# Scores of two units in a row from unit 7 on, in the first batch of an attention and gated-MLP kernel

## Chip and metric

One core of one Trainium2 chip. The metric is device time in microseconds (us) of one execution; "before" is the kernel below, "after" the same kernel with the change. The engines are TensorE (PE; its weight loads PEld), VectorE (DVE), ScalarE (ACT), GpSimd (POOL) and SyncE (SP, which here only issues DMAs).

## What is computed

```python
# q (8,16,384,64), k and v (8,4,384,64): 4 query heads share one k/v head
scores = (1/sqrt(64)) * q @ k.T
attn   = softmax(scores)            # over the 384 keys
x      = (attn @ v)                 # -> (8, 384, 1024)
h      = relu(x @ w_in)             # (8, 384, 1024); u, v = halves of 512
v_n    = (v - mean(v)) / sqrt(var(v) + 1e-6)
v_s    = w_spatial @ v_n + b_spatial   # along the 384 positions
out    = (u * v_s) @ w_out
```

All inputs and the output are float32; the kernel computes its products in float16 with float32 sums.

## The kernel before

**Units.** Work is divided by batch b (8), by *set* s of a batch (6: three blocks of 128 query positions qt, and two halves j of the heads, s = 2 qt + j), and by block kt of 128 keys (3). A *unit* u is one (b, s, kt): u = 18 b + 3 s + kt. `units` (L267) makes its scores: two matmuls of 64 x 128 by 64 x 512 (`sc`, L281), one for each half hh of the array's rows, each into a PSUM bank of its own. The two run at the same time on the two halves of the array. `exp` (L291) then has ACT take the exponential of each into a tile `aT` (L293), which frees the bank. There are three buffers of aT, one for a set.

**What hangs on the units.** When the three units of a set are done, `weigh` (L295) multiplies with v, once for each hh: 12 matmuls (`av`, L301) into one bank; VectorE takes a reciprocal (L315) and a product (`x`, L317), which frees the bank. Here av(s,hh) stands for the one of set s. `x_turn` (L328) transposes x on PE (`xps`, L334, four transposes, two of them of each hh) for the dense part; VectorE copies it out (L218). `q_turn` (L234) does the same for the queries of a set (`qps`, L240), which the scores of that set read as `qT`; `k_turn` (L220) for the keys (`kps`). From batch 2 on, q and k are turned by DMA instead, sent from SP's queue (`q_send`, `k_send`), and from batch 1 on x (`x_send`, L338). The sends of batch 2 are emitted from step 24 on.

**The dense part** is a generator, `gated` (L514), that yields after each matmul: v_part (`pv`, L357, 8 matmuls, then VectorE makes `vr`, L371, and `measure`, L378, its statistics `bn_stats`, L383, right after the next weigh), u_part (`pu`), s_part (`psp`), o_part (`po`). `pour` (L727) takes matmuls from it until a given time in ns is used up; an item ("from", n) stops it until step n. In batch 0 the half v_parts are held so until steps 7, 10, 13, 16, 19.

**Order.** The order on every engine is the order in which this program emits (L53, a manual schedule). In the first 21 units it is one loop with a step per unit:

```python
for u in range(ALONE):                              # ALONE = 21
    if u < TWO or (u - TWO) % 2 == 0:
        pairs = units(u, 1)
        if u >= TWO and u + 1 < ALONE:
            pairs += units(u + 1, 1)
        for pair in pairs:
            exp(*pair)
    spare = 736 if u < TWO else (600 if (u - TWO) % 2 == 0 else 870)
```

After this, in each step: the step's listed work (`todo`; q_turn of set (qt, j) = (1,1) at step 6, (2,0) at 10, (2,1) at 12; x_turn at 5, 9, 12, 15, 18; casts of q on VectorE at step 8; each turn takes 224 off `spare`), the weighs that have become due (for set s of batch 0 at steps 3 s + 4 and 3 s + 5; set 0 both at 4; each takes 372 off), and a pour of what is left of `spare`. From unit 21 on, a second loop takes three units in a row.

**PSUM banks.** All eight banks are shared. `bank` (L79) takes the one that a running estimate expects to be free first:

```python
i = min(range(8), key=done.__getitem__)
t = ps.tile(shape, dtype, name=name, tag=f"bank{i}")
```

The estimate only chooses. On the chip a matmul that writes a bank waits until the engine that reads its earlier content is done.

Of the kernel before, what the change touches and what calls it, by code (L numbers as in the profile page):

```python
# [18 lines left out]
def kernel(  # L19
# [247 lines left out]
    def units(u, count):  # L267
        b, r = divmod(u, UNITS)
        s, kt0 = divmod(r, NT)
        qt, j = divmod(s, 2)  # L270
        kts = range(kt0, kt0 + count)
        if kt0 == 0:
            aTs[b, s] = att.tile([P, NT, 2, G * P], FP16, name=f"aT_{b}_{s}", tag="aT", bufs=3)
        scs = [
            (kt, hh, bank([P, G * P], FP32, f"sc_{b}_{s}_{hh}_{kt}"))
            for hh in range(2)
            for kt in kts
        ]
        for kt, hh, sc in sorted(scs, key=lambda x: x[:2]):
            rows = slice(hh * D, (hh + 1) * D)  # L280
            nc.tensor.matmul(  # L281
                sc,
                kTs[b][rows, j, kt * P : (kt + 1) * P],
                qTs[b, j][rows, qt].rearrange("p (r i c) -> p i r c", r=G, i=G),
                start=True,
                stop=True,
            )
        spend(count * C512 + 186)
        return [(aTs[b, s][:, kt, hh], sc, f"sc_{b}_{s}_{hh}_{kt}") for kt, hh, sc in scs]

    def exp(a, sc, name):  # L291
        reads(act, 480.0, name)
        act.activation(a, sc, AF.Exp, scale=scale)  # L293
# [451 lines left out]
    F = (0.2, 0.3, 0.1, 0.4)  # L745
    owed = 0.0
    halves = {}
    TWO = 13
    for u in range(ALONE):
        if u < TWO or (u - TWO) % 2 == 0:  # L750
            pairs = units(u, 1)
# [5 lines that stand above are left out]
        for f, args in todo.pop(u, []):  # L757
# [282 lines left out]
```

## Time and profile before

| | |
|---|---|
| median of 3 runs | 238.40 us (238.39 to 239.18) |
| the profiled execution | 238.65 us, of which its span 237.1 us |
| busy PE, ACT, VectorE, POOL | 97%, 72%, 61%, 43% |
| granted TensorE clock | 1.00 |
| `sc`, one matmul (288 of them) | 380 ns |
| exponential of 128 x 512 (288) | 617 ns |
| `av`, one matmul (1152) | 193 ns |
| `x`, one product (96) | 424 ns |

The span runs from the first to the last instruction of the program. A row of a timeline gives the start in the span, the length, the engine, the line, and what was written from what; rows with the same line that follow each other are merged, with their number (x4). Rows of PE overlap, since matmuls are pipelined: what a row costs is the distance to the start of the next. Mean lengths in the table overlap too.

The first 21 units lie between 6.2 and 27.8 us. Units 7 to 12 take from 12.5 to 19.2 us.

### The profile page before, as it was taken

The page shows a single profiled execution, that of the slowest core. Times are in us where ns is not written, and L with a number is a line of the kernel's source. Part 1 is how long each engine was busy: PE and PEld are TensorE (multiplying, and loading weights), DVE is VectorE, ACT ScalarE, POOL GpSimd, SP SyncE. Part 2 cuts the span into 40 slices and gives each one's busy share as a digit, 9 for nine tenths or more (in the row PEclk, how much of TensorE's full clock was granted, in tenths as well). Part 3 has the DMA queues.
Part 4 walks back from the last instruction along what each step waited for, and adds up shares of the span by engine and source line. Part 5 has one row for each costly group of instructions (what it writes and reads, how often), then busy time and mean ns, then how long its engine had stood idle before and what let it go on. Part 6 is the DMA issues. An engine that isn't in the chain of part 4 may idle for free.

```text
span 237.1 us, 5954 instructions
## 1 busy us (share of the span) xinstructions
PE 230.4 (97%) x2317; PEld 124.3 (52%) x2317; DVE 143.8 (61%) x382; ACT 170.0 (72%) x350; POOL 102.2 (43%) x149
## 2 busy tenths in 40 slices
PE   7899999999999999999999999999999999999993
PEld 6555655545554545555464555554465455545542
DVE  2668774676447674566646576376744667367561
ACT  2899989959897869977797776986697776401212
POOL 3489493642556442275045800575032500460740
PEclk9999999999999999999999999999999999999999
DMA  6999959999999999699988899479912543240266
GB/s 186 289 300 308 275 152 160 169 317 260 296 211 237 258 351 171 214 199 309 188 257 214 241 214 294 68 271 158 255 27 44 114 164 79 48 177 0 86 229 222
DMA packets 67757, 47.48 MB, mean 200 GB/s; under 512 B 48368, under 2 KB 60576, under 8 KB 67728
## 3 DMA queue, kind: packets, MB, share of 16 engines
q1 hardware_dynamic: 62800, 39.86, 68.9%
q0 software_dynamic: 3952, 6.42, 12.3%
q10 hardware_dynamic: 976, 0.82, 1.1%
q8 instruction: 18, 0.29, 0.5%
q14 instruction: 11, 0.09, 0.1%
HBM read 25.95 MB, written 12.58 MB: 163 GB/s over the span
## 4 chain that ended last, share of the span: by engine, by line
PE 91%; DMA 4%; DVE 2%; issue 0%; ACTq 0%; ACT 0%
PE pu L438 18%; PE pv L357 17%; PE po L496 17%; PE sc L281 15%; PE av L301 14%; PE psp L457 7%; DMA q<-in_q_dram 2%; DMA qT<-q 2%; PE qps L240 1%; PE xps L334 1%; DVE x L317 1%; DVE qT L218 0%; DVE osb L218 0%; DVE q L208 0%; ACTq L124 0%
## 5 line engine op out<-in xcount | busy, mean ns | idle before, releaser
L293 ACT ACTIVATE aT<-sc 128x512 f16<-128x512 f32 x288 | 147.5, 617 | 31.4 <-PE sc L281 30.8
L301 PEld LDWEIGHTS <-aT 128*128 128x128 f16 x1152 | 47.0, 97 | 17.3 <-issue 2.3
L357 PE MATMUL pv<-w_in,xt 128*128 128x512 f16 x192 | 51.0, 380 | 0.1
L301 PE MATMUL av<-v,aT 128*128 128x65 f16 x1152 | 50.5, 193 | 0.1
L496 PE MATMUL po<-w_out,gT 128*128 128x512 f16 (+2 forms) x200 | 50.5, 371 | 0.0
L438 PE MATMUL pu<-xt,w_in 128*128 128x384 f16 x256 | 49.9, 327 | 0.0
L401 POOL TENSOR_SCALAR vn<-vr,rstd,nmr 128x512 f16<-128x512 f32 x23 | 17.6, 779 | 67.0 <-DVE nmr L396 45.6
L474 POOL TENSOR_TENSOR gT<-vs,uT 128x384 f16<-128x384 f32 x31 | 32.4, 1058 | 31.8 <-DVE r_all L315 16.9
L317 DVE TENSOR_TENSOR x<-av,r_all 128x256 f16<-128x256 f32 x96 | 40.7, 424 | 3.3
L281 PE MATMUL sc<-qT,kT 64*128 64x512 f16 x288 | 41.5, 380 | 0.3
L315 DVE RECIPROCAL r_all<-av 128x4 f32<-128x4 f32 x96 | 17.1, 178 | 40.6 <-PE av L301 40.3
L218 DVE COPY osb<-po 128x512 f32<-128x512 f32 (+2 forms) x39 | 26.1, 669 | 16.3 <-PE po L496 16.3
L438 PEld LDWEIGHTS <-w_in 128*128 128x128 f16 x256 | 22.1, 98 | 17.1 <-issue 5.5
L449 ACT ACTIVATE uT<-pu 128x384 f16<-128x384 f32 x32 | 15.8, 495 | 16.0 <-PE pu L438 15.8
L496 PEld LDWEIGHTS <-gT 128*128 128x128 f16 x200 | 17.6, 98 | 17.1 <-issue 3.3
L357 PEld LDWEIGHTS <-xt 128*128 128x128 f16 x192 | 15.8, 97 | 17.8 <-issue 5.5
L281 PEld LDWEIGHTS <-kT 64*128 64x128 f16 x288 | 10.9, 94 | 23.5 <-issue 11.9
L457 PE MATMUL psp<-wsT,vn 128*128 128x384 f16 x96 | 22.2, 327 | 0.0
L469 DVE TENSOR_TENSOR vs<-psp,bias_bc 128x384 f32<-128x384 f32 x32 | 17.6, 552 | 7.1 <-PE psp L457 6.9
L371 DVE TENSOR_SCALAR vr<-pv 128x512 f32<-128x512 f32 x24 | 16.4, 682 | 8.4 <-PE pv L357 8.3
L203 POOL CAST q<-q 128x768 f16<-128x768 f32 x22 | 17.6, 830 | 7.9 <-issue 4.3
L383 DVE BATCH_NORM_STATS2 stats<-vr 128x6 f32<-128x512 f32 x24 | 16.4, 685 | 0.1
(55 smaller groups left out, 103.2 us busy)
## 6 DMA issues: line engine op xcount, KB each, us to landing
out_dram<-osb SPq DMA_DIRECT2D x20, 512.0 KB, 3.9
q<-in_q_dram SPq DMA_DIRECT2D x10, 768.0 KB, 5.7
v_None<-in_v_dram SPq DMA_DIRECT2D x6, 384.0 KB, 7.0
w_in<-in_moe_w_in_dram POOLq DMA_DIRECT2D x4, 512.0 KB, 9.8
k_None<-in_k_dram SPq DMA_DIRECT2D x5, 384.0 KB, 3.8
out_dram<-osb SPq DMA_DIRECT2D x7, 256.0 KB, 2.5
q<-in_q_dram POOLq DMA_DIRECT2D x2, 768.0 KB, 7.6
w_out<-in_moe_w_out_dram POOLq DMA_DIRECT2D x2, 512.0 KB, 9.5
```

The source lines that it names most:

```text
L203: eng.tensor_copy(t16[:, :, :, hh, :], src[:, hh])
L218: (act.copy if eng is act else dve.tensor_copy)(o, i)
L281: nc.tensor.matmul(sc, kTs[b][rows, j, kt * P : (kt + 1) * P], qTs[b, j][rows, qt].rearrange("p (r i c) -> p i r c", r=G, i=G), start=True ...
L293: act.activation(a, sc, AF.Exp, scale=scale)
L301: nc.tensor.matmul(av[:, i * (D + 1) : (i + 1) * (D + 1)], aT[:, kt, hh, i * P : (i + 1) * P], v1[b % 2][:, 2 * j + hh, kt, 0 : D + 1], st ...
L317: dve.tensor_tensor(x16s[b][:, qt, c : c + 256].rearrange("p (i d) -> p i d", i=G), o[:, :, 0:D], r.to_broadcast([P, G, D]), ALU.mult,)
L357: nc.tensor.matmul(pv, xts[b][:, kt, st * P : (st + 1) * P], w_in16[:, kt, DH:DFF], start=(kt == 0), stop=(kt == NK - 1),)
L401: (dve if b == 0 and st == 1 else pool).tensor_scalar(vn, v_r.pop((b, st)), rstd[:, st : st + 1], nmr[:, st : st + 1], op0=ALU.mult, op1=A ...
L438: nc.tensor.matmul(pu[:, 0:S], w_in16[:, kt, m * P : (m + 1) * P], xts[b][:, kt, :], start=(kt == 0), stop=(kt == NK - 1),)
L457: nc.tensor.matmul(psp[:, 0:S], v_n[b, st][:, m * P : (m + 1) * P], wsT16[:, st, :], start=(st == 0), stop=(st == NT - 1),)
L474: pool.tensor_tensor(gT, vs, uT, ALU.mult)
L496: nc.tensor.matmul(po[:, 0:width], gTs[b][:, m, tt * P : (tt + 1) * P], w_out16[:, m, c0 : c0 + width], start=(m == 0), stop=(m == NM - 1),)
```

## The change

```diff
     F = (0.2, 0.3, 0.1, 0.4)
     owed = 0.0
     halves = {}
-    TWO = 13
+    TWO = 7
     for u in range(ALONE):
         if u < TWO or (u - TWO) % 2 == 0:
             pairs = units(u, 1)
```

`TWO` is the first unit that is taken together with its successor. Before, units 0 to 12 are taken one in a step, and 13 and 14, 15 and 16, 17 and 18, 19 and 20 two in the odd steps. After, this begins with 7 and 8: the scores of 8, 10 and 12 are emitted one step earlier, right behind those of 7, 9 and 11, with their four exponentials behind them, and steps 8, 10 and 12 have no scores. The time that is poured in steps 7 to 12 becomes 600 and 870 in turn, where it was 736 each.

## The prediction

> **What bounds the kernel now.** I read the page first, for the engine that carries the chain.
>
> ```profile
> PE 230.4 (97%) x2317; PEld 124.3 (52%) x2317; DVE 143.8 (61%) x382; ACT 170.0 (72%) x350; POOL 102.2 (43%) x149
> ...
> PE 91%; DMA 4%; DVE 2%; issue 0%; ACTq 0%; ACT 0%
> ```
>
> PE is the bound. PE time taken off early reaches the end unless a later wait for something else gives it back; a wait added on PE is added to the end likewise. So I read PE's timeline through steps 7 to 12 (the start of a row minus the start of the next is what it costs on the chain; the second column overlaps):
>
> ```profile
> 12.18 0.40 PE L240 MATMUL qps<-ident,q 128*128 128x128 f16 x4
> 12.51 0.39 PE L281 MATMUL sc<-qT,kT 64*128 64x512 f16 x2
> 12.83 0.54 PE L301 MATMUL av<-v,aT 128*128 128x65 f16 x12
> 13.20 0.59 PE L357 MATMUL pv<-w_in,xt 128*128 128x512 f16 x2
> 13.73 0.39 PE L281 MATMUL sc<-qT,kT 64*128 64x512 f16 x2
> ...
> 18.64 0.39 PE L334 MATMUL xps<-ident,x 128*128 128x128 f16 x4
> 18.87 0.38 PE L357 MATMUL pv<-w_in,xt 128*128 128x512 f16 x1
> 19.18 0.61 PE L281 MATMUL sc<-qT,kT 64*128 64x512 f16 x4
> 19.72 0.54 PE L301 MATMUL av<-v,aT 128*128 128x65 f16 x12
> ```
>
> Units 7 (12.51) and 8 (13.73) stand apart; units 13 and 14 (19.18) stand together. No row has PE idle. Then the engines that free the banks: VectorE's timeline.
>
> ```profile
> 12.61 0.42 DVE L218 COPY qT<-qps 128x512 f16<-128x512 f16 x1 [0.23 <-PE qps L240]
> ...
> 14.85 0.42 DVE L317 TENSOR_TENSOR x<-av,r_all 128x256 f16<-128x256 f32 x1
> ...
> 17.98 0.42 DVE L317 TENSOR_TENSOR x<-av,r_all 128x256 f16<-128x256 f32 x1
> ```
>
> The qps copy holds its bank until 13.03, the two x products hold theirs until 15.27 and 18.40. Today nobody waits for these three; the change moves PE work in front of all of them. ACT in this stretch starts an exponential every 477 ns while it has a backlog (units 3 to 8, up to 14.75), and catches up afterwards (gaps of 0.21 us before unit 9, 0.19 before unit 12): it sets bank times, but not the pace.
>
> **What the change saves.** No instruction is added or removed; the order on PE and what is poured between change. A lone unit costs 0.32 us from its start to the next row (12.51 to 12.83), a pair of units 0.54 (19.18 to 19.72): a second unit in a row is 0.22, so leaving a score group costs 0.32 - 0.22 = 0.10. Two pv products before a score group take 0.53 (13.20 to 13.73), before anything else 0.43 (24.38 to 24.81): entering costs 0.10 too. Three groups go (8, 10 and 12 join 7, 9 and 11): 3 x 0.20 = -0.60 us.
>
> The Trainium skill prices such a break otherwise: its page "TensorE: Matmul & The Clock Gate", section "Single matmul latency", gives a lone warm matmul (398 + N)/2.4 ns, so 398/2.4 = 166 ns beside the streaming. By it three breaks would be an estimated 0.50 us and the sum below 0.10 higher; the row's 0.20 decides.
>
> **What it adds: waits for banks.** I wrote out the loop's order by hand, with the kernel's rule for banks (the one whose planned release is earliest) and its pouring. The same writing-out for the kernel before gives the timeline's order row for row. From step 21 on both orders are the same and each bank follows the same use, so all differences lie in steps 7 to 21:
> 7: sc7 sc8 av(1,0) 2 pv; 8: av(1,1) 2 pv; 9: sc9 sc10 xps; 10: qps av(2,0) 2 pv; 11: sc11 sc12 av(2,1) 1 pv; 12: qps xps 1 pv; 13: sc13 sc14 av(3,0) 2 pv; 14: av(3,1) 2 pv; 16 to 20: pv 2, 1, 1, 1, 1 (before 1, 2, 0, 2, 1).
>
> *Step 7.* Unit 8's second matmul gets the bank of step 6's qps, the only one due. It is due at 12.51 + 0.22 = 12.73; the copy ends at 13.03, and a matmul starts 0.05 after its bank comes free (27.92, where the vr before it ended at 27.19 + 0.68 = 27.87). **+0.35**, start 13.08. Behind it on PE are queued av(1,0) at 13.40, av(1,1) at 13.40 + 0.37 + 0.43 = 14.20, unit 9 at 14.20 + 0.37 + 0.53 = 15.10 (14.96 before).
>
> *Step 9.* Unit 10's second matmul gets av(1,1)'s bank, due 15.32. av(1,0) being later, VectorE has reciprocal 13.97, x 14.19, the two casts of step 8 from 14.53 (0.42), reciprocal of (1,1) 14.95, x 15.17 to 15.59; +0.05. **+0.32**. Then xps 15.96, qps 16.19, av(2,0) 16.42, unit 11 at 17.32 (16.86 before), unit 12 at 17.54. Unit 12 also reads the qT that step 10's qps feeds: PE ends that at 16.59, VectorE copies it behind the xt copy, 16.72 to 17.14, so 0.35 us of cover is left; without it a delay of that copy counts in full.
>
> *Step 12.* av(2,1) starts at 17.86; x ended 1.22 after its av before (17.18 to 18.40), so 19.08. The two pv and the score group that stood between are now one pv: xps starts at 18.69, its third transpose is due at 18.80 and needs that x: 19.13. **+0.33**. Unit 13 at 19.55 (19.18 before).
>
> *Step 18.* Likewise: before, x of (4,1) ended at 25.22 and the third transpose came at 25.31, 0.04 after it could. One pv less stands between: **+0.18**.
>
> *Step 21.* Between unit 19 and unit 21 stand two pv, not three: 2.24 us (25.52 to 27.76) become 2.02. The exponentials of unit 20 end 2.00 and 2.48 after unit 19's start in the records (27.52 and 28.00). Unit 21's second matmul takes the first one's bank (+0.03), unit 22's second the other's: 2.53 against 2.27 (+0.26). Unit 23's second follows step 20's qps, whose copy now stands behind bn_stats (0.69 us, and 0.18 for its aggregate): +0.22. A wait of 0.16 before (27.76 to 27.92, for vr) goes, as that pv ends earlier. **+0.35**.
>
> Sum: -0.60 + 0.35 + 0.32 + 0.33 + 0.18 + 0.35 = **+0.93 us** from unit 24 on, +0.9 in round numbers. Bounds of each wait: nothing, if the planner's bank came free sooner, and the sum of all is 1.53; so -0.60 to +0.93, and I stand at the upper end because the three ends on VectorE are rows, and each lies behind the point where PE will stand.
>
> **What is late next.** From step 21 to 54 us PE's few gaps (30.4, 31.6) wait for work that PE itself started, so they move with it. Then come the queue of SP and PE's own rows:
>
> ```profile
> 31.94 1.41 SPq L586 DMA_TRANSPOSE wsT<-ws  x1
> 33.99 1.24 SPq L341 DMA_TRANSPOSE xt<-x  x1
> ...
> 42.44 0.58 SPq L124 DMA_DIRECT2D q<-in_q_dram  x1
> ...
> 50.10 1.23 SPq L258 DMA_TRANSPOSE qT<-q  x1
> ```
>
> ```profile
> 54.33 0.63 PE L301 MATMUL av<-v,aT 128*128 128x65 f16 x12
> 55.08 1.11 PE L281 MATMUL sc<-qT,kT 64*128 64x512 f16 x6
> ```
>
> The chain has "DMA qT<-q" from 50.10 to 55.04: unit 42 waits there 0.28 us (an av before a score group takes 0.37 + 0.10, so 54.80 was due). Does that wait give back? Its DMA hangs on the q load issued at 42.44, behind the transposes on SP, and these follow the xt send at 33.99, which waits for an x product, so for PE: SP had been free since 33.35. The landing moves with PE; I take nothing back. Bounds: 0 to 0.28 given back. No step of POOL's or SP's program is moved past another: their work is emitted at steps 2, 3 and from 20 on. Afterwards the chain is PE up to the last copy.
>
> **Forecast.** The profiled execution: 238.65 + 0.9 = 239.55 (span 238.0). It stands 0.25 over the median of 238.4; the median goes to 239.3. A measurement of this kernel tells about 0.5%, 1.2 us, from no change (one of three runs was 239.18), so this is slower by less than can be told. Own range: 0.93 - 0.28 = +0.65 to +1.1 (terms rounded up): 239.0 to 239.5.
>
> **Rivals.** *The banks come free in time.* Then only -0.60 is left, 237.8; with the wait at 55.08 shortened too, 237.5. For it: the first transposes and copies on VectorE might be done a little earlier than the records' ends, and ACT's backlog holds no bank that is asked for in steps 7 to 12. Against: three rows with fixed ends, and PE must pass them in order. The Trainium skill's same page, section "The mechanism", says that matmuls start and end strictly in order and only weight loads are pulled ahead: by that rule the av behind the waiting score cannot fill the hole; the trace agrees where unit 21 waits (27.92: the next rows move with it). It decides if the fourth matmul of 12.51's group starts before 12.85.
>
> *The delay runs into the weights' transfer.* POOL issues 1 MB of w_out at 34.14 and 34.88 by its own time, landing at 42.0 and 46.1. Before, the xt transposes are mostly through when it begins at about 36.2 (q1 moved some 550 packets per us from 33 to 37, and under 50 per us from 37 to 41). Started 0.9 later they leave some 500 packets behind it, which at the 210 per us of 41 to 46 is up to 2.4 us for kT, qT and the q load behind them. kT and qT of batch 2 land at 46.5 and 47.0 for use at 48.1, so they are covered; the qT of 55.04 would land up to 2.4 later while PE is there 0.9 later: +0.3 to +1.8 beyond what the forecast has, 239.6 to 241.1, middle 240.4. It decides when xt lands more than 0.9 later than its 40.5. For it: the page's DMA row is full from 37 on. Against: SP itself was held by those same packets until 40.7 before, so the q load need not move more.
>
> **Chances.** Forecast 0.60, banks in time 0.14, transfer 0.26. Of the forecast 0.07 passes +1.2 by the spread of runs; of the banks' rival 0.04 passes -1.2. Faster 0.04, slower 0.26 + 0.07 = 0.33, same 0.63. The range 238.0 to 240.6 leaves out most of the banks' rival (0.11) and the transfer's top (0.09).
>
> **What would show it.** In the changed profile: four scores from 12.5 whose last starts near 13.08; av(1,0) at 13.4; a second such hole near 15.6; an xps near 18.7 with its third transpose 0.33 late; unit 13 near 19.55, unit 21 near 28.3 with two holes, unit 24 near 32.0; the qT landing near 55.9. Wrong: unit 13 before 19.2 (the waits do not bite), or unit 42 later than 56.3 (the transfer).

## The result, and the profile after

| | before | after |
|---|---|---|
| median | 238.44 us (22 runs, 237.77 to 239.42) | 239.21 us (22 runs) |
| ratio after / before | | 1.0029, 95% interval 1.0016 to 1.0043 |
| profiled execution, span | 238.65, 237.1 us | 239.49, 237.9 us |
| first `sc` of unit 7 / unit 24 | 12.51 / 31.07 us | 12.64 / 32.15 us |

One of the 22 executions after took 1292.14 us; the interval leaves it out, the median of the other 21 is 239.17 us, and nothing here explains it. The change makes the kernel slower by 0.16 to 0.43%; the prediction held this to be less than could be told, and with 22 executions of each it can be told. The page of after:

```profile
PE 231.5 (97%) x2317; PEld 123.8 (52%) x2317; DVE 143.2 (60%) x382; ACT 170.2 (72%) x350; POOL 102.1 (43%) x149
...
PE 93%; DVE 2%; DMA 2%; issue 0%; ACTq 0%; ACT 0%
```

Same instructions, and PE busy 1.1 us longer, though it does the same work. PE's timeline of after, from step 6 to unit 13, the transposes of step 18, and unit 21 (start, length, then the row; in brackets how long PE stood idle before the row and what ended that; ... stands for rows left out):

```profile
12.31 0.40 PE L240 MATMUL qps<-ident,q 128*128 128x128 f16 x4
12.64 0.95 PE L281 MATMUL sc<-qT,kT 64*128 64x512 f16 x4
13.53 0.54 PE L301 MATMUL av<-v,aT 128*128 128x65 f16 x12
...
15.22 0.92 PE L281 MATMUL sc<-qT,kT 64*128 64x512 f16 x4
16.07 0.40 PE L334 MATMUL xps<-ident,x 128*128 128x128 f16 x4
16.31 0.39 PE L240 MATMUL qps<-ident,q 128*128 128x128 f16 x4
16.53 0.53 PE L301 MATMUL av<-v,aT 128*128 128x65 f16 x12
16.99 0.60 PE L357 MATMUL pv<-w_in,xt 128*128 128x512 f16 x2
17.53 0.61 PE L281 MATMUL sc<-qT,kT 64*128 64x512 f16 x4
18.07 0.54 PE L301 MATMUL av<-v,aT 128*128 128x65 f16 x12
...
18.88 0.28 PE L334 MATMUL xps<-ident,x 128*128 128x128 f16 x2
19.34 0.28 PE L334 MATMUL xps<-ident,x 128*128 128x128 f16 x2 [0.19 <-DVE x L317]
...
19.77 0.60 PE L281 MATMUL sc<-qT,kT 64*128 64x512 f16 x4
...
25.79 0.58 PE L334 MATMUL xps<-ident,x 128*128 128x128 f16 x4
26.20 0.38 PE L357 MATMUL pv<-w_in,xt 128*128 128x512 f16 x1
...
28.54 1.28 PE L281 MATMUL sc<-qT,kT 64*128 64x512 f16 x6
29.75 0.61 PE L357 MATMUL pv<-w_in,xt 128*128 128x512 f16 x2
```

A group of two units that waits for nothing takes 0.54 us (17.53 to 18.07). The one of units 7 and 8 takes 0.89 (12.64 to 13.53), the one of 9 and 10 takes 0.85 (15.22 to 16.07): these rows have waits in them that count as busy, because the row of the matmul ahead lasts through them. Only the third place, the xps split at 19.34, is written out as a wait. The unsplit xps at 25.79 holds a fourth: 0.41 to the pv behind it, where four transposes took 0.23 before (18.64 to 18.87). Unit 21's row, which merges units 21 to 23, takes 1.21 to the pv behind it; in the kernel before it takes 0.89:

```profile
27.77 0.96 PE L281 MATMUL sc<-qT,kT 64*128 64x512 f16 x6
28.66 0.60 PE L357 MATMUL pv<-w_in,xt 128*128 128x512 f16 x2
```

Against the kernel before and counted from unit 7, unit 24 comes 0.95 us late (1.08 by the clock of the span, of which 0.13 lay ahead of unit 7). Then, from unit 45 to the last matmul, the distance is 0.7: something was given back between 49 and 56 us.

### The profile page after: what moved, and what is told of

The parts are those of the page before. It is cut to its first block, busy times and chain, and to the rows that moved or that the text cites. A ratio compares the mean times of both kernels' runs of the same rounds, so it can differ in the third digit from the quotient of the medians.

```text
span 237.9 us, 5956 instructions
## 1 busy us (share of the span) xinstructions
PE 231.5 (97%) x2317; PEld 123.8 (52%) x2317; DVE 143.2 (60%) x382; ACT 170.2 (72%) x350; POOL 102.1 (43%) x149
## 4 chain that ended last, share of the span: by engine, by line
PE 93%; DVE 2%; DMA 2%; issue 0%; ACTq 0%; ACT 0%
PE pu L438 18%; PE pv L357 18%; PE po L496 18%; PE sc L281 16%; PE av L301 14%; PE psp L457 7%; DMA q<-in_q_dram 2%; PE qps L240 1%; DVE x L317 1%; PE xps L334 1%; DVE qT L218 0%; DVE r_all L315 0%; DVE osb L218 0%; DVE q L208 0%; DVE vr L371 0%
## 5 line engine op out<-in xcount | busy, mean ns | idle before, releaser
L281 PE MATMUL sc<-qT,kT 64*128 64x512 f16 x288 | 42.4, 382 | 0.1
```

What stands on the lines that cost most here:

```text
L281: nc.tensor.matmul(sc, kTs[b][rows, j, kt * P : (kt + 1) * P], qTs[b, j][rows, qt].rearrange("p (r i c) -> p i r c", r=G, i=G), start=True ...
```

## Experiments

What is told of positions comes from the one profiled execution of each run. In some kernels the lines are moved by one. Of each edit the lines that matter are shown; ... stands for lines left out.

**Banks and pouring, apart and together.** The running estimate that hands out banks may book an `av`'s bank longer, in the first 21 steps only:

```diff
+    hold = [500.0]
...
-            done[taken.pop(name)] = clock[eng]
+            done[taken.pop(name)] = clock[eng] + (hold[0] if name.startswith("av") else 0.0)
...
+    hold[0] = 0.0
```

(the last line stands behind the first loop), and the time poured in paired steps may be split more evenly:

```diff
-        spare = 736 if u < TWO else (600 if (u - TWO) % 2 == 0 else 870)
+        spare = 736 if u < TWO else (700 if (u - TWO) % 2 == 0 else 770)
```

The changed kernel with the first:

> The changed kernel, with one thing altered: in the first 21 steps the running estimate books an av's bank 500 ns longer, so that other banks are handed out. Order, pouring and instruction counts stay. Theory (waits for banks on PE cost more than the three joined groups save): the last score of unit 8 and of unit 10 no longer wait (0.35 and 0.30 us go), the third transpose of step 12's xps, the one of step 18 and unit 21's waits stay; between unit 7 and unit 24 the kernel is 0.6 us shorter than the changed one, which leaves it 0.3 us longer than the kernel before. At the end about +0.3 or less against before: 238.4 to 238.8. Rival (the pouring in steps 7 to 12 is to blame, banks are not): no difference from the changed kernel, 239.2.

with the second:

> The changed kernel, with one thing altered: 700 and 770 ns are poured in the two kinds of paired steps, where it was 600 and 870. Theory: the two bank waits of steps 7 and 9 stay (0.35 and 0.30), more pv stands ahead of the x that steps 12 and 18 wait for and ahead of unit 21, so the wait of step 12 falls from 0.35 to 0.12, that of step 18 goes, and those of unit 21 fall from about 0.5 to the 0.15 of before; a new 0.12 in front of av(2,1). Unit 24 is 0.65 us earlier than in the changed kernel and 0.3 later than before. Rival (only the banks matter): as the changed kernel, 239.2.

with both:

> The changed kernel with both alterations: an av's bank booked 500 ns longer, and 700 and 770 ns poured. Theory: the waits left in steps 7 to 21 are 0.1 to 0.15 each, and the joined groups now show: unit 24 is 0.45 us earlier than before (1.4 earlier than in the changed kernel). At the end: the wait for v of batch 2 near 51 us, which has its own time, and the one for qT near 55 us take back what is early, so 238.2 to 238.5, the same as before to 0.1%. Rival (what is won early reaches the end): 238.0, that is 0.45 below before, with no longer wait at 51 or 55 us.

and the kernel before with both:

> The kernel before (units 7 to 12 alone) with both alterations of the run with both. Theory: its banks were in time already and its steps from 13 on are paired as before, so unit 24 moves by less than 0.1 us and the time is that of before, 238.4. Rival (the alterations are worth something by themselves, not through the joined units): earlier by up to the 1.4 us that both give on the changed kernel.

| | median, us | ratio to before (95%) | landing of w_in, 2nd part | fifth pv starts, and its wait | unit 24 | unit 24 less landing |
|---|---|---|---|---|---|---|
| before | 238.44 | | 16.44 | 16.55, 0 | 31.07 | 14.63 |
| after | 239.21 | 1.0016 to 1.0043 | 16.64 | 16.99, 0.1 | 32.15 | 15.51 |
| banks | 239.41 | 1.0033 to 1.0067 | 16.66 | 16.71, 0.91 | 31.86 | 15.20 |
| pouring | 239.00 | 1.0012 to 1.0038 | 16.49 | 16.53, 0.33 | 30.97 | 14.48 |
| both | 238.56 | 0.9994 to 1.0033 | 16.56 | 16.60, 0.58 | 31.04 | 14.48 |
| before, both | 238.48 | 0.9981 to 1.0018 | 16.11 | 16.15, 0.14 | 30.65 | 14.55 |

(A wait is the distance from the av's last matmul to the pv, less that of the kernel before. The 0.1 of the changed kernel is not a wait for the landing, which came 0.35 earlier.) The bank waits of units 8 and 10 are gone in "both". In "banks" unit 8's is down from 0.35 to 0.06 us, but unit 10's only from 0.30 to 0.22: its group still takes 0.76 instead of 0.54 (14.01 to 14.77), where none was expected. And the time did not come down: "banks" misses its 238.4 to 238.8, and by the medians it is no faster than the changed kernel. "Both" misses as well: its unit 24 was to come 0.45 us before that of the kernel before, and comes 0.03 before it. PE's timeline of "banks" shows why:

```profile
14.01 0.82 PE L282 MATMUL sc<-qT,kT 64*128 64x512 f16 x4
14.77 0.40 PE L335 MATMUL xps<-ident,x 128*128 128x128 f16 x4
...
15.44 0.52 PE L302 MATMUL av<-v,aT 128*128 128x65 f16 x12
16.71 0.59 PE L358 MATMUL pv<-w_in,xt 128*128 128x512 f16 x2 [0.74 <-DMA w_in<-in_moe_w_in_dram]
```

The fifth pv of batch 0 reads the second part of w_in, and in every kernel whose PE gets there before the landing it starts 0.04 to 0.05 us after it, whatever the kernel did before. In the chain of waits of "both", from 5 to 22 us, the piece that ends at the landing reaches back to the cast of v ahead of the load on POOL:

```profile
7.66 0.48 POOL v L192
8.13 8.43 DMA w_in<-in_moe_w_in_dram
16.56 0.04 issue
16.60 0.38 PE pv L358
```

So the landing is a floor under step 10, and the kernel before stands 0.06 above it (16.55 against 16.44 + 0.05). What PE wins in steps 7 to 9 is lost there; what it loses counts. The last column takes the floor out: after it, "pouring" and "both" are 0.07 better than the control, "before, both", which sat on the floor too; "banks" is 0.65 worse, the changed kernel 0.96. The control itself stays within 0.08 of the kernel before.

Two things follow. The waits behind step 10 (steps 12, 18 and 21: 0.35, 0.18 and 0.32) cost 0.65, the 0.20 that the third joined group saves already taken off, and they all but go when the pouring is evened: 600 and 870 put less pv between an av and the transposes that read its x, and less between units 19 and 21. The bank waits of steps 7 and 9 cost the other 0.31: their 0.65 less the 0.40 of two joined groups, on top of the 0.06 that the kernel before stands above the floor. The rival that only banks matter falls, by the positions and by the medians (239.41 for "banks", 238.56 for "both"). That only pouring matters falls by the positions: "pouring" has both bank waits in its profile (12.41 and 15.07 us), hidden there because its PE came to unit 7 early, at 11.82, and met the floor anyway. The medians do not settle this half, as the intervals of "pouring" and "both" overlap. The profiled execution of "pouring" took 238.35 us, its median is 239.00, 0.12 to 0.38% above before; that fits executions that come to unit 7 later and show the bank waits, which is argued, not shown.

**Moving the floor.** The load of w_in's second part is issued one cast earlier on POOL:

```diff
-    cast_v(0, pool, (0,))
     load_w_in(1, 4, 8)
+    cast_v(0, pool, (0,))
```

In the kernel with both alterations, and in the kernel before:

> The run with both alterations showed a wait of its own in step 10: the fifth pv of batch 0 starts 0.05 us after the second part of w_in has landed (near 16.5), whatever PE won before. Here the kernel with both alterations issues that load on POOL ahead of a cast of v, so some 0.6 us earlier; nothing else. New theory (that landing is a floor under step 10, and PE of the kernel before stands almost on it): the landing moves to near 15.9, the wait shrinks by as much, and units 21 and 24 come 0.3 to 0.6 us earlier than in the run with both. At the end up to as much, less what the v of batch 2 (near 50.6) takes back: 238.0 to 238.5. Rival (something else holds step 10): the pv starts near 16.6 as it did.

> The kernel before with the same earlier load and nothing else. Theory of the floor: PE of the kernel before reaches the fifth pv 0.0 to 0.3 us after or before the landing, depending on when its first loads land, so it wins 0.0 to 0.3 us by unit 24 and 0 to 0.1% at the end: 238.1 to 238.5. Rival (the floor holds both kernels alike): it wins the same 0.3 to 0.6 as the kernel with both alterations.

Both missed, and were the slowest of all: 240.21 us (ratio 1.0035 to 1.0114) and 240.64 (1.0051 to 1.0122). The profiled executions took 239.31 and 239.63, about a microsecond less than these medians, so they show where a part of the loss lies and not all of it. The load landed at 17.18 and 16.45, no earlier. What moved was another: the q load for the casts of step 8 landed at 15.40 and 15.51, 2 us after its 13.35 of before. VectorE's timeline and PE's in the kernel before with the earlier load:

```profile
15.54 0.49 DVE L208 CAST q<-q 128x256 f16<-128x256 f32 x2 [1.57 <-DMA q<-in_q_dram]
15.95 0.17 DVE L315 RECIPROCAL r_all<-av 128x4 f32<-128x4 f32 x1
16.16 0.42 DVE L317 TENSOR_TENSOR x<-av,r_all 128x256 f16<-128x256 f32 x1
```

```profile
15.19 0.29 PE L334 MATMUL xps<-ident,x 128*128 128x128 f16 x2
16.64 0.28 PE L334 MATMUL xps<-ident,x 128*128 128x128 f16 x2 [1.16 <-DVE x L317]
```

The cast waits for q, the reciprocal of av(1,1) stands behind it, and PE's transposes wait for that x. The page of before has the DMA row at 9 tenths through this stretch, and here an earlier issue of one load only made another later. The floor could not be moved this way, so whether lifting it alone is worth something stays open.

**One group alone, behind the floor.**

```diff
-    TWO = 7
+    TWO = 11
```

> TWO = 11: only unit 12 is joined to unit 11, behind step 10. One group less (-0.20), the third transpose of step 12's xps late (+0.34), step 18 and unit 21 as before. Theory: unit 24 is 0.14 us later than before, unit 13 too, and the time 238.5 to 238.7. Rival (each joined group is worth its 0.20): 238.2.

It took 238.57 us, ratio 0.9974 to 1.0023. Unit 24 less the landing is 14.69, that is 0.14 above "before, both" on the same floor, as expected: its xps waits 0.35 for the x of av(2,1) (two transposes take 0.46 where they take 0.11 alone), and the group saves 0.20:

```profile
18.33 0.28 PE L334 MATMUL xps<-ident,x 128*128 128x128 f16 x2
18.79 0.29 PE L334 MATMUL xps<-ident,x 128*128 128x128 f16 x2 [0.18 <-DVE x L317]
```

The median cannot tell it from no change, nor from the rival's 238.2; the position can.

**The waits worked out.** More banks booked longer, an even pouring, and the pv half that meets w_in held one step longer:

```diff
+    hold = {"sc": 500.0, "av": 300.0, "qp": 800.0, "xp": 300.0}
...
-            done[taken.pop(name)] = clock[eng]
+            done[taken.pop(name)] = clock[eng] + hold.get(name[:2], 0.0)
...
-                    yield ("from", 6 * st + 10)
+                    yield ("from", (11, 17, 22)[st])
-        spare = 736 if u < TWO else (600 if (u - TWO) % 2 == 0 else 870)
+        spare = 736 if u < TWO else 800
...
+    hold.clear()
```

> The changed kernel with all waits of steps 7 to 21 worked out of it that can be: the running estimate books banks of scores, av, qps and xps 500, 300, 800 and 300 ns longer in the first 21 steps, 800 ns are poured in each paired step, and the later halves of the first three v_parts are held until steps 11, 17 and 22 (10, 16, 22 before). Theory: bank waits in steps 7 and 9 go, pv no longer meets the w_in landing in step 10, the waits left are about 0.1 in steps 11, 12 and 21; unit 24 and unit 27 are 0.5 us earlier than before. At the end the v of batch 2 takes back 0.2 to 0.4 of it: 238.1 to 238.4. Rival (all is won): 237.9.

238.29 us, ratio 0.9976 to 1.0015: not told from before. Here unit 9 starts 2.25 us after unit 7 (12.11 to 14.36) where it was 2.45, exactly one group's 0.20 less and no wait. The fifth pv starts at 17.42, a microsecond after the landing at 16.33: the floor is no longer met. And yet unit 24 lies 0.16 later, counted from unit 7, than before. PE's timeline of this kernel, and a part of its chain between 5 and 20 us:

```profile
12.11 0.61 PE L282 MATMUL sc<-qT,kT 64*128 64x512 f16 x4
...
14.36 0.63 PE L282 MATMUL sc<-qT,kT 64*128 64x512 f16 x4
...
16.05 0.91 PE L282 MATMUL sc<-qT,kT 64*128 64x512 f16 x4
17.06 0.52 PE L302 MATMUL av<-v,aT 128*128 128x65 f16 x12
```

```profile
6.17 0.04 issue
6.21 0.42 PE sc L282 x2
6.63 10.39 ACT aT L294 x21
17.02 0.04 issue
17.06 0.52 PE av L302 x12
```

The exponentials, 21 in a row without a gap on ACT, are the next limit. PE waits for them in unit 12 and in the av behind it (the group at 16.05 takes 1.01 us instead of 0.54). The forecast that unit 24 would come 0.5 us earlier missed this. So there are two limits close under the kernel before in this stretch, one of DMA and one of ACT, and joined score groups move neither.

**A delay by itself.** 17 matmuls of 128 x 128 on PE in step 20 of the kernel before:

```diff
+        if u == 20:
+            i = min(range(8), key=done.__getitem__)
+            hole = ps.tile([P, P], FP32, name="hole", tag=f"bank{i}")
+            for _ in range(17):
+                nc.tensor.matmul(hole, zero16, zero16, start=True, stop=True)
```

> The kernel before with 17 matmuls of 128 x 128 that nobody reads, put on PE in step 20: a pure delay of 0.95 us (17 x 0.056), after the landing of w_in and ahead of unit 21. No other order changes. Theory (a delay of PE after step 10 reaches the end, but for what the waits at 51 and 55 us give back): unit 24 is 0.95 us later by the landing of w_in, 0.0 to 0.5 of it is given back by unit 42, and the time is +0.5 to +0.95: 238.9 to 239.4, like the changed kernel's. Rival (later waits have slack for it, the changed kernel's loss is elsewhere): 238.4 to 238.6.

239.36 us, ratio 1.0024 to 1.0060 to before. Counted from its w_in landing, unit 24 comes at 15.35, 0.72 above before's 14.63 and 0.80 above the control. The effect on the median, 0.8 us against the 238.57 of the kernel before in the same set of runs, is of that size and of that of the changed kernel: what is lost behind step 10 reaches the end. In this profile nothing was given back at 51 us, on the contrary:

```profile
50.59 1.03 PE L496 MATMUL po<-w_out,gT 128*128 128x512 f16 x4
52.24 0.53 PE L301 MATMUL av<-v,aT 128*128 128x65 f16 x12 [0.62 <-POOL v L191]
```

The first av of batch 2 waits 0.79 for the cast of v, whose load landed at 51.24. In the kernel before it was 50.02 (wait 0.27), after 49.66 (none). The order of these three landings follows that of w_out's second part (47.80, 46.07 and 43.08 us), but this is no rule: in "both" w_out is through at 45.89 and v lands at 49.38, earlier than in the changed kernel. What sets v's landing stays open.

## Why the prediction was right

The median was 239.21 where 239.3 was forecast, and up to unit 24 the mechanism was the forecast one. By its steps:

- *Saving of 0.20 for each joined group.* Right: 0.20 for unit 9 in the schedule with the waits worked out, where nothing waits. The estimate of 0.166 that the prediction took from the Trainium skill (page "TensorE: Matmul & The Clock Gate", section "Single matmul latency") is less than that. The Trainium skill's page "TensorEngine Tiling (Array Packing)", section "Key Properties", says that a change of tiling mode drains TensorE. A score group has such a change at both its borders, two half arrays inside and the whole array outside; that the 0.20 is the price of draining is shown by no run here.
- *Step 7, +0.35:* 0.35 (the fourth matmul at 13.22 instead of 12.87). *Step 9, +0.32:* 0.30. *Step 12, +0.33:* 0.35. *Step 18, +0.18:* 0.18. *Step 21, +0.35:* 0.32, by the two groups shown (1.21 less 0.89). Unit 24: +0.93 was the sum, 0.95 was measured. The terms as measured add to 0.90; the other 0.05 lies in step 10, where qps and av take 0.68 to the pv (16.31 to 16.99) and took 0.62 before (15.93 to 16.55).
- *What is late next: "The landing moves with PE; I take nothing back."* Wrong, and the step of the prediction that failed. The wait at 55.08 was not for DMA any more: qT landed at 53.04, 2 us earlier than before and not 0.9 later, though its chain began later on PE: the q load behind it was issued at 44.15 instead of 42.44 and landed at 48.39 instead of 48.85. That gave no time back, since the 0.19 saved at unit 42's first matmul was lost again inside units 42 to 44, which wait for banks; the chain of after between 55 and 57 us has the fourth of their matmuls behind vr:

```profile
55.13 0.19 DVE r_all L315
55.33 0.02 issue
55.35 0.42 DVE x L317
55.77 0.61 DVE vr L371
56.38 0.04 issue
56.43 0.60 PE sc L281 x3
```

  And 0.27 was given back at a wait that the prediction had not listed: the first av of batch 2 in the kernel before, 51.02, for a cast of v. (The control, "before, both", has no wait there, so it need not stand in every execution of the kernel before.) The two profiled executions differ by 0.84, where +0.9 was forecast. That is in part luck: the 0.27 given back, which was forecast as nothing, stands against 0.13 lost ahead of unit 7, which no step had forecast.
- *The rival "the banks come free in time", 237.8.* Its condition failed in the changed kernel (the fourth matmul came at 13.22), and when its mechanism was tried its price was wrong too. With the bank waits mostly out the kernel took 239.41, and with pouring evened as well 238.56: step 10's floor was in the trace of before (landing 16.44, pv 16.55) and was not looked for, because nobody waited there yet. A step that stands 0.06 behind a landing has no wait to show.
- *The rival "the delay runs into the weights' transfer", from the point that xt lands more than 0.9 later.* xt landed 3.3 later (43.82 against 40.54), so the point was passed; kT of batch 2 landed earlier all the same (45.85 against 46.51). The packets left behind are not a fixed cost: w_out itself was through 3 us earlier, at 43.08. In the changed kernel both parts of w_out were issued ahead of that xt (33.84 and 34.58, then 35.08), in the kernel before behind it (33.99, then 34.14 and 34.88). The point was badly chosen.

## To carry to other kernels

Where an order is written by hand against a few shared banks, joining two groups moves the second one in front of whatever was about to free its bank: find each bank's previous user and its end in the trace before pricing the joined group. And before counting a gain in the first part of a kernel, list what lands there and when, also where nobody waits today: a stretch can rest on a load and on an engine's backlog at once, and then only losses pass through.

## What the runs showed of the hardware that was not expected

- The second part of w_in landed between 16.11 and 16.66 us in the nine kernels with the old order of loads, though it was issued between 7.25 and 8.52: here, where the DMA row is full, the time of issue hardly counted. Issued before a cast it landed at 16.45 and 17.18, and the q load of step 8 landed 2 us later.
- In the kernel before ACT starts an exponential of 128 x 512 every 477 ns as long as it has a backlog, while the rows grow from 597 to 805 ns: the length of a row in a backlog is not its cost.
